# Dropping row tiles in AV slots without scores, and moving two stores to another queue, in a sliding-window attention and GELU kernel

## Chip, cores, metric

One core of a Trainium2 chip. The time is the device time of the core in microseconds (us). A kernel is run several times beside the kernel before on the same chip. A time is the median of a kernel's runs unless a mean is named; "span" is first to last instruction, about 1.7 us less than the time.

## Reference, cut

```python
# q, k, v: (4, 8, 768, 64); n_sink = 4; window = 128
scores = q @ k.transpose(0, 1, 3, 2) / sqrt(64)
keep = (key position < 4) | ((0 <= query - key) & (query - key < 128))
a = softmax(where(keep, scores, -1e9))
x = (a @ v) as (3072, 512)
out = gelu(x @ w_in) @ w_out        # w_in (512, 2048), w_out (2048, 512)
```

## The kernel before

The 3072 rows are worked on in six chunks of 512. While chunk c runs through the two weight matmuls (`gemm1`, `gemm2`), the attention of chunk c + 1 is put between the matmuls of `gemm2`, in slots: scores of two units, then their masks, and four slots later AV (the product of the attention weights with the values) of the two units. A unit is a pair of heads in a group of 256 queries; two groups make a chunk, three groups a batch. Chunk 0 and the attention of chunk 1 are in a hand-made list, the prologue.

AV of two units at once: the window part takes 128 rows of the array. The four sink keys (the first four keys of a batch, which every query sees) are a second, small part per head. For a pair of units it uses row tiles: the array is split into two halves of 64 rows that work at the same time, with unit one's sinks on one half and unit two's on the other. Going from 128 to 64 rows or back is a "mode change" below.

```python
    def av(*units, spare=False, fill=0):
        ets = [ET.pop(u) for u in units]
        pos = [bank2() if spare else bank() for _ in units]
        tiled = len(units) > 1
        ...
        def sinks(n, e):
            g, p = units[n]
            rows = slice(HP * (p // 2), HP * (p // 2 + 1)) if tiled else slice(0, P)
            nc.tensor.matmul(                                     # L526
                pos[n][:, e * PV : (e + 1) * PV],
                lhsT=ETS[g][rows, e * P : (e + 1) * P],
                rhs=VS[g // NBP % 2][rows, 2 * p : 2 * p + 2, :]...
                start=not tiled and e == 0, stop=tiled, ...)
        for n, (g, p) in enumerate(units):
            sunk = g % NBP > 0          # the first group of a batch has no separate sinks
            for e in range(2):
                if sunk and not tiled:
                    sinks(n, e)
                ... four (or three) window matmuls ...            # L546
        if tiled:
            for e in range(2):
                for n, (g, p) in enumerate(units):
                    if g % NBP > 0:
                        sinks(n, e)
        ... per unit: reciprocal (L564), product into xg (L568) on VectorE ...

    def pair_slots(c, weights):
        us = units(c)
        ...
        for n in range(0, len(us), 2):
            two = us[n : n + 2]
            slots[n + 4].append((0, lambda two=two: av(*two)))
            slots[n].append((2, lambda two=two: [scores(*u) for u in two]))   # L473
            slots[n].append((4, lambda two=two: [mask_scores(*u) for u in two]))
```

Eight units a chunk: AV lies in slots 4, 6, 8 and 10, scores in slots 0, 2, 4 and 6. So slots 8 and 10 hold AV alone.

The stores of the last chunk, at the end of `gemm2_mm`:

```python
            eng = nc.scalar if part[0] == DM // 2 else nc.sync
            eng.dma_start(out=out[r0 : r0 + P, cols], in_=osb[:, cols])
```

Row blocks 0 to 2 are stored whole, block 3 in three parts, the middle one from ScalarE's queue.

The softmax here doesn't subtract the row's maximum and nothing guards it: scores larger than these inputs give would overflow.

## Time and profile before

| | before |
|---|---|
| time, median of 3 runs | 226.35 us |
| span of the profiled run | 224.0 us |
| TensorE busy | 97% |
| AV slot without scores, first AV to first L682, earlier / later of a chunk | 0.80 / 0.90 us |
| end wait for the last store to SP's first drain | 0.43 us |

A row of the timeline is a run of equal instructions: start, length, engine, line, tiles, count. TensorE's records overlap, so only differences of starts are durations. The rows themselves are in the prediction.

### The profile page before, as it was taken

What the parts mean: (1) busy time and instruction counts of PE and PEld (TensorE: products, weight loads), DVE (VectorE), ACT (ScalarE), POOL (GpSimd) and SP (SyncE); (2) the same over time, 40 slices, a digit from 0 to 9 for tenths busy, and PEclk for the clock granted to TensorE, in tenths of its full rate; (3) what the DMA queues carried; (4) which work ended last, traced back from release to release, by engine and by line L of the source; (5) the groups of instructions that cost most, each with busy time, mean ns of one, the idle gap of its engine ahead of it and who ended that gap; (6) DMA issues with size and microseconds to landing.
All of it is one profiled execution on the core that took longest, in us unless ns stands there. A gap on an engine that the chain in (4) does not pass through costs nothing.

```text
span 224.0 us, 4231 instructions
## 1 busy us (share of the span) xinstructions
PE 216.8 (97%) x1705; PEld 114.9 (51%) x1705; DVE 111.7 (50%) x267; ACT 120.8 (54%) x148; POOL 51.8 (23%) x95
## 2 busy tenths in 40 slices
PE   7898999999999999999999999999999999999994
PEld 2455887554544465444455444455444465444453
DVE  4437725786690287480297580297550397100121
ACT  2367675866165974065973165963157972278000
POOL 8475513466220011310011400011400011300000
PEclk9999999999999999999999999999999999999999
DMA  6999999999487994477997487986582027500112
GB/s 169 290 348 388 354 352 290 360 273 320 149 188 147 282 276 98 94 151 137 302 255 98 94 171 162 295 217 109 105 170 41 3 47 98 122 17 3 47 47 94
DMA packets 70194, 40.11 MB, mean 179 GB/s; under 512 B 27168, under 2 KB 64416, under 8 KB 70176
## 3 DMA queue, kind: packets, MB, share of 16 engines
q1 hardware_dynamic: 68112, 34.55, 61.0%
q0 software_dynamic: 1920, 5.25, 9.4%
q8 instruction: 13, 0.21, 0.4%
q10 hardware_dynamic: 144, 0.07, 0.1%
q14 instruction: 5, 0.04, 0.1%
HBM read 27.26 MB, written 6.29 MB: 150 GB/s over the span
## 4 chain that ended last, share of the span: by engine, by line
PE 86%; ACT 5%; DVE 3%; DMA 2%; issue 1%; SPq 0%; DVEq 0%
PE po L682 34%; PE big L613 29%; PE bank L546 4%; PE big L473 4%; PE big L646 4%; ACT et L482 3%; DMA st<-in_q_dram 2%; PE po L646 2%; PE bank L613 2%; PE bank L526 1%; ACT L713 1%; DVE xg L568 1%; PE qkps L363 1%; PE big L363 1%; PE big L462 1%
## 5 line engine op out<-in xcount | busy, mean ns | idle before, releaser
L682 PE MATMUL po<-WOUT,gt 128*128 128x512 bf16 (+2 forms) x416 | 89.8, 363 | 0.1
L613 PE MATMUL big<-xt,WIN 128*128 128x512 bf16 x300 | 66.1, 379 | 0.0
L682 PEld LDWEIGHTS <-gt 128*128 128x128 bf16 x416 | 36.9, 98 | 39.5 <-issue 3.0
L632 ACT ACTIVATE gt<-big 128x1024 bf16<-128x1024 f32 (+1 forms) x32 | 30.6, 969 | 44.7 <-PE big L613 44.7
L613 PEld LDWEIGHTS <-WIN 128*128 128x128 bf16 x320 | 31.4, 98 | 37.7
L482 ACT ACTIVATE et<-big 128x1024 bf16<-128x1024 f32 (+1 forms) x48 | 43.4, 952 | 11.7 <-PE big L473 11.5
L697 POOL DMA_DIRECT2D out_dram<-osb x40 | 22.9, 578 | 107.6 <-DVE rz L564 79.8
L490 DVE TENSOR_TENSOR et<-et,mask 128x1024 bf16<-128x1024 bf16 x31 | 22.3, 729 | 33.6 <-ACT et L482 33.2
L272 DVE COPY osb<-po 128x512 f32<-128x512 f32 (+2 forms) x25 | 16.1, 646 | 38.4 <-PE po L682 38.4
L568 DVE TENSOR_TENSOR xg<-bank,rz 128x256 bf16<-128x256 f32 x44 | 18.7, 425 | 1.5
L546 PEld LDWEIGHTS <-et 128*128 128x128 bf16 x352 | 14.6, 97 | 5.0 <-issue 0.2
L272 DVE CAST vo<-st 64x512 bf16<-64x512 f32 x36 | 16.4, 456 | 0.4
L473 PE MATMUL big<-qt,kt 64*128 64x128 bf16 (+1 forms) x256 | 15.5, 238 | 0.8 <-ACT et L482 0.2
L626 ACT ACTIVATE gt<-big 128x1024 bf16<-128x1024 f32 (+1 forms) x8 | 9.8, 1240 | 11.0 <-PE big L613 11.0
L546 PE MATMUL bank<-vo,et 128*128 128x65 bf16 x324 | 14.2, 193 | 0.0
L646 PEld LDWEIGHTS <-WIN 128*128 128x128 bf16 x128 | 12.3, 98 | 1.5
L473 PEld LDWEIGHTS <-kt 64*128 64x128 bf16 x256 | 8.6, 94 | 7.7 <-issue 6.0
L497 DVE TENSOR_TENSOR et<-et,mask 128x768 bf16<-128x768 bf16 x12 | 6.9, 581 | 9.8 <-ACT et L482 9.5
L713 ACT ACT_TABLE_LOAD x9 | 11.5, 1283 | 0.2
L564 DVE RECIPROCAL rz<-bank 128x4 f32<-128x4 f32 x44 | 7.7, 175 | 5.9 <-PE bank L526 3.2
L646 PE MATMUL big<-xt,WIN 128*128 128x256 bf16 x80 | 10.3, 273 | 0.0
L272 DVE CAST k<-st 128x1024 bf16<-128x1024 f32 (+1 forms) x12 | 8.1, 672 | 3.2 <-DMA st<-in_k_dram 3.2
(86 smaller groups left out, 138.2 us busy)
## 6 DMA issues: line engine op xcount, KB each, us to landing
st<-in_k_dram SPq DMA_DIRECT2D x12, 512.0 KB, 7.1
st<-in_q_dram SPq DMA_DIRECT2D x12, 512.0 KB, 7.3
st<-in_v_dram SPq DMA_DIRECT2D x12, 512.0 KB, 7.3
out_dram<-osb POOLq DMA_DIRECT2D x40, 128.0 KB, 2.7
st<-in_moe_w_in_dram SPq DMA_DIRECT2D x8, 512.0 KB, 9.6
st<-in_moe_w_out_dram SPq DMA_DIRECT2D x8, 512.0 KB, 8.9
out_dram<-osb SPq DMA_DIRECT2D x3, 256.0 KB, 2.0
kt<-k SPq DMA_TRANSPOSE x16, 3.0
```

Of the source, the lines that this page charges most:

```text
L272: eng.tensor_copy(out=out, in_=in_)
L473: nc.tensor.matmul(ps[:, hl, c : c + n * P], lhsT=kt(gk, p, ek, rows), rhs=qt(g, p, e, n, rows), start=not add, stop=True, skip_group_chec ...
L482: nc.scalar.activation(out=et[:, :, c0:], in_=ps[:, :, c0:], func=AF.Exp, scale=att_scale)
L490: nc.vector.tensor_tensor(out=et.rearrange("p h (e n) -> p (h e) n", e=2), in0=et.rearrange("p h (e n) -> p (h e) n", e=2), in1=mask.unsqu ...
L546: nc.tensor.matmul(pos[n][:, e * PV + hl * DV : e * PV + (hl + 1) * DV], lhsT=ets[n][:, hl, c : c + P], rhs=vo[:, h, :], start=e == 0 and ...
L568: nc.vector.tensor_tensor(out=XG[g][:, :, 2 * p : 2 * p + 2, :], in0=po[:, 0 : 2 * PV].rearrange("p (e h c) -> p e h c", e=2, h=2)[:, :, : ...
L613: nc.tensor.matmul(outs[a], lhsT=WIN[:, t, ts(f, P)], rhs=XT[c][:, :, t, :], start=(t == 0), stop=(t == NKT - 1),)
L632: nc.scalar.activation(out=gt.rearrange("k a n -> k (a n)"), in_=src, func=AF.Gelu)
L646: nc.tensor.matmul(out4[a], lhsT=WIN[:, t, ts(f, P)], rhs=XT[c][:, 2 * half : 2 * half + 2, t, :], start=(t == 0), stop=(t == NKT - 1), sk ...
L682: nc.tensor.matmul(po, lhsT=GT[c, f // 4][:, f % 4, ts(m, P)], rhs=WOUT[:, f, cols], start=(f == 0), stop=(f == NFT - 1),)
L697: nc.gpsimd.dma_start(out=out[r0 : r0 + P, :].rearrange("(s r) c -> r s c", r=2)[r], in_=osb[HP * r : HP * (r + 1), :],)
L713: nc.scalar.activation(out=warm[:, 1:2], in_=warm[:, 0:1], func=func)
```

## The change

Its intent: in slots with scores the sinks share their change to 64 rows with the scores, which need it too; in slots without, the change of mode stands there for the sinks alone, so drop the row tiles. And move two stores off the hardware queues.

```diff
-    ("s", [3,3], ""), ("av", [3,0,2], ""), ...
+    ("s", [3,3], ""), ("av", [3,0,2], "U"), ...
-    ("av", [3,1,3], ""), ...
+    ("av", [3,1,3], "U"), ...
-            eng = nc.scalar if part[0] == DM // 2 else nc.sync
+            eng = nc.gpsimd if m < 2 else nc.scalar if part[0] == DM // 2 else nc.sync
-            slots[n + 4].append((0, lambda two=two: av(*two)))
+            groups = [two] if n + 4 < len(us) else [[u] for u in two]
+            slots[n + 4].append((0, lambda groups=groups: [av(*us) for us in groups]))
# in run(): an "av" entry marked "U" calls av once per unit, too
```

## The prediction

> **What bounds the kernel now.** I read the page first, then the chain of work that ended last, then the PE timeline round every AV block, last the end of the program. The page:
>
> ```profile
> PE 216.8 (97%) x1705; PEld 114.9 (51%) x1705; DVE 111.7 (50%) x267; ACT 120.8 (54%) x148; POOL 51.8 (23%) x95
> PEclk9999999999999999999999999999999999999999
> PE 86%; ACT 5%; DVE 3%; DMA 2%; issue 1%; SPq 0%; DVEq 0%
> ```
>
> TensorE is busy for 97% of the 224.0 us, holds 86% of the chain, and has its full clock in every slice. So a nanosecond taken out of the PE stream inside chunks 1 to 4 should reach the end, unless another engine then holds PE up. The records overlap (a 128x512 matmul is written as 380 ns but a new one starts every 216 ns), so I work with starts, never with durations. The PE timeline of the first two slots that the change rewrites (AV, no scores):
>
> ```profile
> 84.75 0.65 PE L546 MATMUL bank<-vo,et 128*128 128x65 bf16 x16
> 85.33 0.29 PE L526 MATMUL bank<-vsk,ets 64*128 64x130 bf16 x4
> 85.54 1.90 PE L682 MATMUL po<-WOUT,gt 128*128 128x512 bf16 x8
> 87.28 0.74 PE L546 MATMUL bank<-vo,et 128*128 128x65 bf16 x16
> 87.96 0.29 PE L526 MATMUL bank<-vsk,ets 64*128 64x130 bf16 x4
> 88.18 0.60 PE L682 MATMUL po<-WOUT,gt 128*128 128x512 bf16 x2
> ```
>
> L546 is AV, L526 the sink part of AV on 64 rows, L682 the second matmul of the MoE, on 128 rows. From the first start of L546 to the first of L682 the slot takes 0.80 us, and the later one 0.90 us. For contrast, one of the two slots of chunk 3's loop whose batch has no separate sinks, so that it never leaves 128 rows:
>
> ```profile
> 151.58 0.53 PE L546 MATMUL bank<-vo,et 128*128 128x65 bf16 x12
> 151.94 1.89 PE L682 MATMUL po<-WOUT,gt 128*128 128x512 bf16 x8
> ```
>
> 0.36 us for 12 matmuls: 30 ns each, and nothing lost on either side. Single records of the trace say where the 0.80 goes: starts are 29 to 35 ns apart in AV, then 124 ns from the last AV to the first sink (29 is normal, so 95 lost), 70 ns for four sinks (two and two, partners 3 to 4 ns apart), 149 ns to the first L682 (57 is normal after 130 columns, so 92 lost), and 226 instead of 216 ns inside the first L682: 10 more. In the later slot 128 ns lie between the eighth and the ninth AV. There PE's queue has a separate semaphore instruction of 51 ns: the ninth weight load waits for two engines (DVE and ACT), and one instruction holds one wait.
>
> In the slots that hold scores as well, the switch into 64 rows is shared:
>
> ```profile
> 79.22 0.65 PE L546 MATMUL bank<-vo,et 128*128 128x65 bf16 x16
> 79.80 0.29 PE L526 MATMUL bank<-vsk,ets 64*128 64x130 bf16 x4
> 79.92 0.60 PE L473 MATMUL big<-qt,kt 64*128 64x128 bf16 x12
> 80.46 1.68 PE L682 MATMUL po<-WOUT,gt 128*128 128x512 bf16 x7
> ```
>
> L473 follows L526 after 53 ns, with no loss: the scores would need 64 rows anyway. This is why the change leaves those slots alone.
>
> **What the Trainium skill says.** "TensorEngine Tiling (Array Packing)", Key Properties: "Changing tiling mode (not just tile) drains the TensorE". The trace agrees: 92 to 98 ns lost at every change between 128 and 64 rows, nothing without one. "TensorE: Matmul & The Clock Gate", Part 3: matmuls in different row tiles run at the same time, starts about 4 ns apart. The trace agrees with 3 to 4 ns; that concurrency is what the change gives up. "Perfetto Trace Analysis", Sequencer-only Instruction: such a record starts when its semaphores are satisfied, the wait itself is not in it. The trace agrees: the end wait for the last store starts at 222.60 us, its last increment lands at 222.59. I use this below.
>
> **The change, part by part.** (1) The untiled pair. The early untiled pair of the same kernel, in the prologue, is the ruler:
>
> ```profile
> 24.04 0.22 PE L526 MATMUL po<-vsk,ets 128*128 128x130 bf16 x1
> 24.09 0.28 PE L546 MATMUL po<-vo,et 128*128 128x65 bf16 x4
> 24.21 0.22 PE L526 MATMUL po<-vsk,ets 128*128 128x130 bf16 x1
> ...
> 24.74 0.28 PE L588 MATMUL bank<-ident,xg 128*128 128x128 bf16 x2
> ```
>
> From 24.04 to 24.74 us: 0.706 us by the single records, for 4 sinks at 57 and 16 AV at 30 ns. So the instruction count stays, the sinks cost 228 instead of 70 ns, and both switches go. The earlier slot goes from 799 + 10 to 706, a gain of 0.103 us. In the later one the built program's double wait is gone too (the sink's load takes the DVE wait, the AV load the ACT wait): 895 + 10 to 706, a gain of 0.199 us. Together 0.302 us a chunk.
>
> How many chunks: the rule is all slots from the fifth unit on, in the loops that prepare chunks 2 to 5. Those are the second groups, 5, 7, 9 and 11. Group 9 starts a batch (9 is a multiple of 3) and has no separate sinks; its order in the built program is the same before and after. So three chunks, at 84.7, 117.8 and 184.4 us: 3 x 0.302 = **0.91 us**. The two marked prologue entries are of group 3, also a batch start: no TensorE or DVE instruction moves, worth 0. Groups whose prologue AV does lose two switches (44.45 and 48.61 us) are left tiled.
>
> (2) The two stores. Where they run is nothing: they leave at 211 and 214 us and have landed by 216.5. But completion semaphores of the hardware queues go round in eight lanes, and SP waits for the lanes in fixed order at the end. Its end records and waits:
>
> ```profile
> L869 SPq EVENT_SEMAPHORE  x11: 17/28/28, 221.4 to 223.9; - x11
> L869 SPq DRAIN  x3: 7/7/13, 223.0 to 223.4; - x3
> SPq L869 <- DMA out_dram<-osb: 1.1, 2, 0.7
> ```
>
> The built program shows the last store on lane 1 before, the third of nine waits. In the trace it ends at 222.60; six waits that have long been satisfied follow one after the other, 61 ns each (222.668, .729, .789, .850, .909, .971), and only then the drain at 223.036. With two stores fewer on the hardware queues the last store has lane 7, the ninth wait: the others are done while it is in flight. Worth 6 x 61 = **0.37 us**, all at the end of the chain.
>
> Sum: 0.91 + 0.37 = 1.28 us, from 226.35 to **225.1 us**, 0.57%.
>
> **The rivals.** (a) The bank takes the switch's place. In the later slot the second unit needs the bank that DVE's xg of the slot before frees; that ends at 87.473, set by ACT's exp and DVE's mask and copy, which do not move. A PE wait on such an xg started 53 ns after its end at 153.8, so the load can start at 87.526; PE would come at 87.53. It just fits. If it did not, 0.05 us in each of three chunks: 225.2. (b) The PE gain is absorbed at a chunk's edge. The first matmul there needs xg's DMA transpose: issued 89.50, some 3.1 us to landing, so 92.6 against a start at 93.15. The change brings xg forward by about 0.5 us, as unit by unit DVE starts earlier, and PE by 0.3, so the slack grows. PE does wait for ACT at the head of a chunk (L473, 0.13 to 0.39 us), but that ACT chain (last Gelu, table load, two exps) starts at PE's last first-matmul and moves with it. Against this rival, then; if true, only the tail is left, 226.0. (c) The stores hurt. GpSimd's stores take 2.7 us to landing against 1.8 on SP, and its drain lasted 4.27 us after its last store. From 214.1 us that ends near 218.4, over 3 us before the last landing. A third store would have come close, two do not. If it were wrong, some 1 us is lost: 226. (d) The end waits stay in the chain although the lane changes: then 225.4.
>
> **Range and chances.** The terms come from the same trace with starts that repeat within 3 ns in three chunks; the three runs before spread by 0.35 us, more than any term's doubt. With (a), (d) and the spread, 224.7 to 225.7 should hold it. 2% would be 4.5 us, over three times what I can find, and nothing that the change adds costs as much: faster by over 2% 0.01, within 2% 0.98, slower 0.01.
>
> **What would show it.** Right: in the PE timeline the six slots start with L526 on 128 rows and take 0.70 to 0.72 us to the first L682; the PE chain arrives 0.3 us earlier after each of three chunks and not after chunk 3's loop; the span falls to about 222.7; the last store's end wait is followed by the drain within 0.1 us. Wrong: a gap before the second unit's sink in the later slot (a); PE waits longer at L613 or L473 at chunk heads (b); a GpSimd semaphore or GpSimd itself comes last at the end (c); six 61 ns steps still after the last landing (d).

## The result, and the profile after

| | before | after |
|---|---|---|
| median of 6 runs | 226.32 us | 224.99 us |
| lowest to highest | 225.66 to 226.73 | 224.48 to 225.75 |
| span of the profiled run | 224.0 us | 223.6 us |
| AV slots without scores | 0.80 / 0.90 us | 0.71 / 0.71 to 0.72 us |
| end wait for the last store to first drain | 0.43 us | 0.07 us |

The ratio is 0.9945, with a 95% interval of 0.9919 to 0.9971: about 1.25 us less, where 1.28 was predicted; the interval reaches from 0.7 to 1.8 us. A ratio is the mean time of one kernel's runs over that of the other's of the same rounds, so not quite the ratio of the medians quoted.

The PE timeline of the same two slots after (the first two that the change rewrites):

```profile
85.59 0.22 PE L526 MATMUL bank<-vsk,ets 128*128 128x130 bf16 x1
85.64 0.28 PE L546 MATMUL bank<-vo,et 128*128 128x65 bf16 x4
...
86.30 1.89 PE L682 MATMUL po<-WOUT,gt 128*128 128x512 bf16 x8
88.02 0.22 PE L526 MATMUL bank<-vsk,ets 128*128 128x130 bf16 x1
...
88.74 0.81 PE L682 MATMUL po<-WOUT,gt 128*128 128x512 bf16 x3
```

L526 now reads 128*128: the whole array. 85.59 to 86.30 and 88.02 to 88.74 are 0.71 and 0.72 us. The six slots took 708, 717, 709, 713, 711 and 714 ns by the single records; before they took 799, 895, 799, 892, 799 and 893. With the first L682 at 216 to 217 instead of 226 to 227 ns, that is 0.87 us saved, where 0.91 was predicted.

The end of the program after, in the rows of the end line and of SP's waits (count, shortest, median and longest in ns, first and last start):

```profile
L875 SPq EVENT_SEMAPHORE  x11: 17/28/28, 221.4 to 223.5; - x11
L875 SPq DRAIN  x3: 7/7/13, 222.6 to 223.0; - x3
SPq L875 <- DMA out_dram<-osb: 0.7, 1, 0.7
```

SP waits once for a store, not twice, and its first drain, at 223.0 before, is at 222.6. By the single records the nine waits start at 221.38, then in steps of some 61 ns to 221.82, and the last one, lane 7, at 222.584; the drain follows at 222.649. TensorE's last matmul started at 220.45 before and 220.43 after, so nearly all of the 0.4 us by which these two profiled spans differ is this end.

That is the puzzle of this pair of traces: TensorE saved 0.87 us in its slots, yet reached its end at the same moment. Where it was given back is in a part of the prologue that the change does not touch. The timeline near 44 us, before:

```profile
43.48 0.69 DVE L490 TENSOR_TENSOR et<-et,mask 128x1024 bf16<-128x1024 bf16 x1 [0.43 <-ACT et L482]
43.94 0.70 PE L546 MATMUL bank<-vo,et 128*128 128x65 bf16 x16
44.50 1.04 POOL L272 CAST WOUT<-st 128x1024 bf16<-128x1024 f32 x1 [1.15 <-DMA st<-in_moe_w_out_dram]
```

and after:

```profile
42.10 2.38 POOL L272 CAST WOUT<-st 128x1024 bf16<-128x1024 f32 x2 [2.26 <-DMA st<-in_moe_w_out_dram]
43.62 1.40 DVE L490 TENSOR_TENSOR et<-et,mask 128x1024 bf16<-128x1024 bf16 x1 [0.43 <-ACT et L482]
44.08 0.41 PE L546 MATMUL bank<-vo,et 128*128 128x65 bf16 x8
45.07 0.41 PE L546 MATMUL bank<-vo,et 128*128 128x65 bf16 x8 [0.58 <-DVE et L490]
```

GpSimd casts weights when their load lands. In the run before, the second of these casts came after DVE's mask (44.50). In the run after, its load landed earlier (43.32 us, against 44.45 before), and the cast ran from 43.44 to 44.48, when the mask started at 43.62. The mask then took 1.40 instead of 0.69 us, and AV of group 2 waited for it between its eighth and its ninth matmul (776 ns between their starts, 72 before). The first L613 after the prologue starts at 59.995 instead of 59.148: 0.85 us late. From there the starts of the later chunks tell the gain: 93.151 became 93.706 (0.29 won), 126.207 became 126.475 (0.29), 159.018 became 159.287 (nothing, as predicted for that chunk), 192.798 became 192.779 (0.29). Two of the six runs after had a span of 222.8, which is what the prediction's 222.7 asks for; the profiled one was not among them.

"SBUF — State Buffer", section Who interferes with whom, of the Trainium skill states that a DVE instruction with two inputs in SBUF and a GpSimd instruction that reads SBUF exclude each other, and that the second to start waits for the first to end. The traces agree in both directions: mask first (before, 41.76), the cast takes 1.38 instead of 1.04 us; cast first (after, 43.44), the mask takes 1.40 instead of 0.69.

### The profile page after: what moved, and what is told of

It is laid out like the page before. It is cut to its first block, busy times and chain, and to the rows that moved or that the text cites.

```text
span 223.6 us, 4228 instructions
## 1 busy us (share of the span) xinstructions
PE 215.2 (96%) x1705; PEld 114.7 (51%) x1705; DVE 112.8 (50%) x267; ACT 120.8 (54%) x148; POOL 52.3 (23%) x97
## 4 chain that ended last, share of the span: by engine, by line
PE 85%; ACT 5%; DVE 4%; DMA 2%; issue 1%; SPq 0%; DVEq 0%
PE po L682 34%; PE big L613 29%; PE bank L546 4%; PE big L473 4%; PE big L646 4%; ACT et L482 3%; DMA st<-in_q_dram 2%; PE po L646 2%; PE bank L613 2%; PE bank L526 1%; ACT L715 1%; DVE et L490 1%; DVE xg L568 1%; PE qkps L363 1%; PE big L462 1%
## 5 line engine op out<-in xcount | busy, mean ns | idle before, releaser
L682 PE MATMUL po<-WOUT,gt 128*128 128x512 bf16 (+2 forms) x416 | 89.8, 364 | 0.1
L613 PE MATMUL big<-xt,WIN 128*128 128x512 bf16 x300 | 66.1, 379 | 0.0
L682 PEld LDWEIGHTS <-gt 128*128 128x128 bf16 x416 | 36.9, 98 | 38.9 <-issue 3.0
L613 PEld LDWEIGHTS <-WIN 128*128 128x128 bf16 x320 | 31.3, 98 | 37.8
L568 DVE TENSOR_TENSOR xg<-bank,rz 128x256 bf16<-128x256 f32 x44 | 18.7, 424 | 1.5
L546 PEld LDWEIGHTS <-et 128*128 128x128 bf16 x352 | 15.2, 97 | 4.9 <-DVE et L490 0.7
L546 PE MATMUL bank<-vo,et 128*128 128x65 bf16 x324 | 15.1, 193 | 0.6 <-DVE et L490 0.6
```

The costliest lines, as they stand in the source:

```text
L546: nc.tensor.matmul(pos[n][:, e * PV + hl * DV : e * PV + (hl + 1) * DV], lhsT=ets[n][:, hl, c : c + P], rhs=vo[:, h, :], start=e == 0 and ...
L568: nc.vector.tensor_tensor(out=XG[g][:, :, 2 * p : 2 * p + 2, :], in0=po[:, 0 : 2 * PV].rearrange("p (e h c) -> p e h c", e=2, h=2)[:, :, : ...
L613: nc.tensor.matmul(outs[a], lhsT=WIN[:, t, ts(f, P)], rhs=XT[c][:, :, t, :], start=(t == 0), stop=(t == NKT - 1),)
L682: nc.tensor.matmul(po, lhsT=GT[c, f // 4][:, f % 4, ts(m, P)], rhs=WOUT[:, f, cols], start=(f == 0), stop=(f == NFT - 1),)
```

## The experiments

Twelve runs, all correct.

**1. Each half alone, and tiles dropped everywhere.** `e1_slots_only` is the change without its store line:

```diff
-            eng = nc.gpsimd if m < 2 else nc.scalar if part[0] == DM // 2 else nc.sync
+            eng = nc.scalar if part[0] == DM // 2 else nc.sync
```

> The slot half of the change alone, the stores as before. My theory (six slots without scores lose their two row-mode changes, three of them also the double wait): 0.91 us less than the kernel before, the six slots at 0.70 to 0.72 us from the first sink to the first L682, and six satisfied waits of 61 ns still standing after the last landing. Rival (the gain comes mainly from the stores): within 0.3 us of before.

Measured: ratio 0.9959 (0.9944 to 0.9974), 0.93 us less than before by the ratio; the six slots took 709 to 718 ns. The single records still show the last store's wait at 221.965, six more of some 61 ns, and the drain at 222.398: 0.43 us. As the theory says.

`e2_stores_only` is the kernel before with only the store line changed:

```diff
-            eng = nc.scalar if part[0] == DM // 2 else nc.sync
+            eng = nc.gpsimd if m < 2 else nc.scalar if part[0] == DM // 2 else nc.sync
```

> The store half alone, the slots as before. My theory (the last store moves from lane 1 to lane 7, so six end waits of 61 ns are done while it flies): 0.37 us less than before, all of it between the last landing and the first drain (0.43 us before, 0.07 us after). Rival (the stores do nothing): 0.0 us and 0.43 us in that place.

Measured: ratio 0.9982 (0.9967 to 0.9997), 0.41 us less by the ratio. From the last store's wait (223.438) to the drain (223.503) 0.07 us. The two halves add up: 0.93 + 0.41 = 1.34 against 1.25 for both, within the intervals.

`e3_lanes_split`, on the kernel before, asks whether GpSimd has anything to do with it:

```diff
-            eng.dma_start(out=out[r0 : r0 + P, cols], in_=osb[:, cols])
+            for w0 in range(part[0], part[0] + part[1], P if m < 2 else part[1]):
+                cs = slice(w0, w0 + (P if m < 2 else part[1]))
+                eng.dma_start(out=out[r0 : r0 + P, cs], in_=osb[:, cs])
```

> The kernel before, no store on GpSimd; the first two stores of the last chunk are cut into four each on the sync queue, so that six more hardware DMAs turn the last store to lane 7. If the lane alone is the cause: the same 0.37 us as the stores half, 0.07 us from the last landing to the first drain. Rival (GpSimd's queue or a shorter sync queue is the cause): no gain, or a loss from eight issues of 0.33 us.

Measured: the profile did what the lane theory says (its rows of the end line and of SP's waits):

```profile
L871 SPq DRAIN  x3: 7/7/7, 223.3 to 223.6; - x3
SPq L871 <- DMA out_dram<-osb: 0.7, 1, 0.7
```

The last store's wait is at 223.214, the drain at 223.279: 0.07 us, without any store on GpSimd. But the ratio was 1.0007 (0.9994 to 1.0021): no gain in time. Its profiled run, at a span of 224.2, is explained: the prologue's AV stall was there (694 ns), and 224.0 + 0.61 (its first L613 at 59.758) - 0.40 gives 224.2. The five other runs had 224.5 to 224.8, more than that, and nothing of them but the span is known. So the cause of the missing gain was open; run `e12_split_stores` and point 5 below take it up.

`e4_untile_all`, on the changed kernel, drops the tiles in all pairs:

```diff
-            groups = [two] if n + 4 < len(us) else [[u] for u in two]
+            groups = [[u] for u in two]
-                for two in [[u] for u in us] if "U" in op[2] else [us]:
+                for two in [[u] for u in us]:
```

> The changed kernel with every AV pair untiled, also in the slots that hold scores. My theory (there the row tiles share their mode change with the scores): the six such slots with sinks in the loops go from 0.70 us (first AV to first score) to about 0.80 us, 0.097 us each or 0.58 us in all; the two pairs of group 2 in the prologue gain 0.1 us each; so some 0.4 us slower than the changed kernel, about 0.9 us faster than before. Rival (untiled AV is simply faster anywhere): a further 0.5 us gain over the changed kernel.

Measured: ratio 0.9967 (0.9953 to 0.9982), 0.85 us under before by the means (0.75 by the ratio), so some 0.4 us of the change's 1.25 us was lost (the changed kernel itself did not run on this chip). Its PE timeline of a slot with scores:

```profile
78.95 0.22 PE L526 MATMUL bank<-vsk,ets 128*128 128x130 bf16 x1
...
79.54 0.28 PE L546 MATMUL bank<-vo,et 128*128 128x65 bf16 x4
79.75 0.61 PE L473 MATMUL big<-qt,kt 64*128 64x128 bf16 x12
```

From the first AV instruction to the first score 0.80 us; with tiles (79.22 to 79.92 in the kernel before) it was 0.70. By the single records 805 to 807 ns in all six such slots with sinks, 702 to 705 with tiles. The mode change does not go away, it moves in front of the scores, and the sinks lose their concurrency. Untiled AV is not faster as such; the rival falls.

**2. Is it the mode change, or only the order unit by unit?** `e6_tiles_one_by_one`, on `e1_slots_only`, keeps the units apart in these slots, but with row tiles:

```diff
-        tiled = len(units) > 1
+        tiled = rowtile or len(units) > 1
-            ... [av(*us) for us in groups]
+            ... [av(*us, rowtile=True) for us in groups]   # rowtile: new argument of av, False otherwise
```

(The flag reaches the slots with scores as well; their pairs are tiled anyway.)

> The kernel before, in the slots without scores each unit of the pair alone, but still with row tiles: four mode changes a slot instead of two, and no two sinks at the same time. My theory (about 95 ns for each change, 57 ns for a sink alone): each unit takes 207 + 124 + 57 + 149 = 537 ns, so 1.08 us from the first AV to the first L682 in the earlier slot (0.80 before) and 1.17 in the later one, which keeps its double wait (0.90 before); over six slots 1.65 us slower than before. Rival (the gain of the change is one of order, unit by unit, and not of the modes): faster than before by up to 0.9 us.

Measured: ratio 1.0058 (1.0038 to 1.0079), 1.3 us slower. The later slot of the first pair of slots in its PE timeline:

```profile
87.58 0.40 PE L546 MATMUL bank<-vo,et 128*128 128x65 bf16 x8
87.91 0.28 PE L526 MATMUL bank<-vsk,ets 64*128 64x130 bf16 x2
88.13 0.42 PE L546 MATMUL bank<-vo,et 128*128 128x65 bf16 x8
88.48 0.28 PE L526 MATMUL bank<-vsk,ets 64*128 64x130 bf16 x2
88.70 0.39 PE L682 MATMUL po<-WOUT,gt 128*128 128x512 bf16 x1
```

1.12 us. In the earlier slot the trace lacks one matmul's record; counted in, it is 1.12 as well. TensorE's last matmul started 1.61 us later than in the kernel before, with the same prologue (first L613 at 59.128 and 59.148); 1.65 was expected. The time grew by less than that, as more of the runs before than of these lay in the longer group of spans (experiment 3). The parts were a little off: a sink alone took 66 to 68 ns on 64 rows, not 57, and the double wait, still in the built program, cost nothing here: the ninth AV follows its sink after 149 ns in both slots, the same as a mode change without it. The record shows why: the separate semaphore instruction of the later slot ran at 87.489 us, 39 ns after the end of the xg that it waits for, and so before even the first AV of its slot (87.577). It was done long before PE reached the ninth AV.

**3. The prologue.** Four runs on one chip. `e5_after_again` is the changed kernel.

> The changed kernel again, as the ruler for the three runs beside it. Expected 1.28 us under the kernel before. My theory for its spread (0.8 us wide, as wide as that of the kernel before): in the prologue a mask of DVE (two inputs in SBUF) meets a GpSimd cast of weights, which starts whenever its load lands; whichever starts first blocks the other, and where the cast was first, AV of group 2 waits up to 0.7 us for its second unit. So the gap between the eighth and the ninth AV near 44 us should be one of 0.03 to 0.8 us, and large just where a cast started before the mask did. Rival (the spread is noise of the clock or of the end): no such gap goes with a long run.

Measured: ratio 0.9954 (0.9935 to 0.9973). The six spans fell into two groups: 222.7 and 222.8, and four times 223.6. The profiled run was one of the long ones, with 775 ns before the ninth AV, and again its cast (43.43) started before the mask (43.61), which took 1.40 us. The nine profiles with uncut casts agree with the expectation: in the five where a cast was well under way when the mask of group 2 began (changed kernel, `e1_slots_only`, `e2_stores_only`, `e3_lanes_split`, this one) the gap was 246 to 780 ns; in the other four, where the cast came later, had ended, or was in its last 0.1 us (`e4_untile_all`), it was at most 90.

`e7_untile_group2` takes the change one step further, in the two places that the prediction had named as left out:

```diff
-    ("av", [2,0,2], ""), ... ("av", [2,1,3], "")
+    ("av", [2,0,2], "U"), ... ("av", [2,1,3], "U")
```

> The changed kernel, with the two AV pairs of group 2 in the prologue untiled as well; they stand between weight matmuls, without scores. My theory: each loses two mode changes, 0.80 + 0.01 to 0.71 us, together 0.20 us less than the changed kernel. Rival (the prologue is bound by loads, DVE or ACT there, and the gain is given back at once): the first L613 after the prologue starts no earlier, 0.0 us.

Measured: ratio 0.9933 (0.9916 to 0.9949), means 0.54 us under `e5_after_again`. Spans 222.4, 222.5, 222.5 and 223.0 to 223.2. Its PE timeline of the two pairs:

```profile
43.97 0.22 PE L526 MATMUL bank<-vsk,ets 128*128 128x130 bf16 x1
...
44.68 1.03 PE L682 MATMUL po<-WOUT,gt 128*128 128x512 bf16 x3
...
48.04 0.22 PE L526 MATMUL bank<-vsk,ets 128*128 128x130 bf16 x1
...
48.75 0.38 PE L682 MATMUL po<-WOUT,gt 128*128 128x512 bf16 x1
```

0.71 us each, where the kernel before took 0.85 and 0.80. In this trace, as in that of the kernel before, the cast came after the mask, and the two are alike up to 44 us: the first L613 starts at 58.924 against 59.148, 0.22 earlier. So the 0.20 foreseen is there; the shorter group of spans, 222.4 to 222.5 against 222.7 to 222.8, says the same. The rest of the 0.54 between the means may be how many runs fell into the longer group (three of six against four).

`e8_quarter_casts`, on the changed kernel, cuts the three late casts:

```diff
-            copy(eng, WOUT[:, j * NW : (j + 1) * NW, :], st.rearrange("p (f c) -> p f c", c=DM))
+            ... for j in (4, 5, 6) four copies of [128, 256], else as before
```

> The changed kernel, with the three late weight casts of GpSimd cut into four quarters each (256 instead of 1024 elements, so about 0.3 instead of 1.04 us). If a mask is blocked for as long as the GpSimd instruction that was there first: no mask of the prologue after 40 us takes over 1.1 us (1.4 before), the gap before the ninth AV stays under 0.4 us, and the runs' spread falls to about half, the mean 0.2 to 0.4 us under the changed kernel. Rival (GpSimd and DVE share in small steps, so that only the total overlap counts): masks as long as before, no change in the spread.

Measured: ratio 0.9954 (0.9933 to 0.9974). In the timeline the mask of group 2 met a quarter and waited for that quarter only:

```profile
41.85 5.65 POOL L272 CAST WOUT<-st 128x256 bf16<-128x256 f32 x12 [1.65 <-DMA st<-in_moe_w_out_dram]
43.56 0.81 DVE L496 TENSOR_TENSOR et<-et,mask 128x1024 bf16<-128x1024 bf16 x1 [0.42 <-ACT et L488]
```

0.81 us, with a gap of 189 ns before the ninth AV: what "blocked for as long as the instruction that was there first" asks for, and not what sharing in small steps would give. But the run did not show the smaller spread: four spans of 222.8 to 223.1, and two of 223.7 and 224.2; the mean (224.99) is that of `e5_after_again` (225.05). The block is shown. It is not the whole of the spread: in the profile of `e11_sync_stores` below, with the same cut casts and at most 88 ns between two AV of group 2, the first gemm1 matmul still came at 60.24 us, 1.35 us later than in that of `e9_quarters_group2` (58.89). There TensorE itself waited twice for weights that GpSimd had still to cast:

```profile
47.95 0.59 PE L688 MATMUL po<-WOUT,gt 128*128 128x512 bf16 x2 [0.53 <-POOL WOUT L272]
49.04 0.59 PE L688 MATMUL po<-WOUT,gt 128*128 128x512 bf16 x2 [0.50 <-POOL WOUT L272]
```

The load behind these casts landed at 46.27, in `e9_quarters_group2` at 45.34.

`e9_quarters_group2` has both edits, those of `e7_untile_group2` and `e8_quarter_casts`, on the changed kernel.

> Quarters of the casts and group 2 untiled together, on the changed kernel: the candidate that should beat both kernels. Sum of the two expectations: 0.4 to 0.6 us under the changed kernel, 1.7 to 1.9 us under the kernel before, so about 224.4 us. If the two gains lie on the same wait, only the larger of them.

Measured: ratio 0.9932 (0.9916 to 0.9947), median 224.41, spans 222.5 to 222.8 and one of 223.3. It beats both kernels: 1.52 us under the kernel before and 0.56 under the changed kernel beside it (means), at the top of the range expected for the second, short of it for the first. It is no better than `e7_untile_group2` (mean 224.49 against 224.51), so the quarters are worth nothing that these runs can show, and the simpler of the two is to be preferred.

**4. The end again, on `e9_quarters_group2`.** `e11_sync_stores` puts all stores back as they were before; `e12_split_stores` cuts the first two as `e3_lanes_split` did; `e10_three_stores` has `m < 3` in place of `m < 2`.

```diff
 # e11_sync_stores
-            eng = nc.gpsimd if m < 2 else nc.scalar if part[0] == DM // 2 else nc.sync
+            eng = nc.scalar if part[0] == DM // 2 else nc.sync
 # e12_split_stores: that line as in e11, and the loop of e3_lanes_split around the store
 # e10_three_stores
-            eng = nc.gpsimd if m < 2 else ...
+            eng = nc.gpsimd if m < 3 else ...
```

> On the same kernel: all three whole stores back on the sync queue, last store on lane 1. Expected 0.37 us slower than with two stores on GpSimd (mean 224.49 then), 0.43 us from last landing to first drain.

Measured: ratio 0.9956 (0.9935 to 0.9976), 0.43 us from the last store's wait (222.838) to the drain (223.270), as expected. Its mean of 225.17 is 0.68 us above that of `e9_quarters_group2`, where 0.37 was expected, but on another chip, and two of its six spans (223.9 and 224.2, the others 223.1 to 223.2) were long; its profile is one of them.

> On the same kernel: no store on GpSimd, the first two stores cut into four each on the sync queue, last store on lane 7. The first run of this kind on the kernel before showed 0.07 us from last landing to drain as foreseen, yet no gain in time (+0.1 us, where -0.37 was expected). If that was the prologue's spread, this run is 0.37 us faster than the run beside it with whole stores on the sync queue. If cutting the stores costs 0.4 us somewhere, it is the same as that run, and its profile must show the place.

Measured: ratio 0.9934 (0.9911 to 0.9957), the mean 0.49 us under `e11_sync_stores` beside it; 0.07 us from wait (222.069) to drain (222.134). That is what the lane's gain without GpSimd should look like, but the two intervals overlap, so the time alone does not show it; point 5 does. In the profiled run the last store itself landed 1.82 us after it was issued, 0.26 us more than the 1.56 in the changed kernel's profile. Such a late landing could have hidden part of the gain in the unprofiled runs of `e3_lanes_split`, but no run shows that it did, and those runs stay unexplained.

> On the kernel with quarter casts and group 2 untiled: a third store on GpSimd. My theory: the last store now has lane 6, so one satisfied wait follows it, 0.06 us more than with two stores. GpSimd's drain, which ended 4.05 us after its last store began (214.69 to 218.74), would end near 221.4, just short of the last landing near 221.5: no more cost, but no room left. Rival: the drain comes last and the end moves out by 0.5 us or more.

Measured: ratio 0.9951 (0.9930 to 0.9972). The last store's wait (lane 6) starts at 221.854, one wait and 0.13 us later comes the drain. GpSimd's own drain ended at 221.486, 0.37 us before that: no cost, as expected, and no room left. The time differs from that of `e9_quarters_group2` by more than the 0.06 us expected, but on another chip and within the spread that the prologue makes, so nothing follows from it.

**5. All traces between the same two marks.** The two marks are the first gemm1 matmul after the prologue (L613, or L619 where casts are cut) and TensorE's last matmul. They split each profiled span, in us:

| run | to the first gemm1 | from there to the last matmul | from there to the end |
|---|---|---|---|
| before | 59.15 | 161.30 | 3.54 |
| `e2_stores_only` | 59.98 | 161.31 | 3.16 |
| `e3_lanes_split` | 59.76 | 161.30 | 3.15 |
| `e1_slots_only` | 59.37 | 160.44 | 3.52 |
| after | 60.00 | 160.44 | 3.17 |
| `e11_sync_stores` | 60.24 | 160.45 | 3.52 |
| `e12_split_stores` | 59.21 | 160.45 | 3.42 |

Every trace with the slot change as it stands, also those of `e5_after_again`, `e7_untile_group2`, `e8_quarter_casts`, `e9_quarters_group2` and `e10_three_stores`, has 160.44 to 160.45 us in the middle: some 0.86 us less than before, whatever the prologue did. The end is shorter by 0.37 to 0.39 us wherever the last store has lane 7, without GpSimd too (`e3_lanes_split`); only `e12_split_stores` loses 0.26 us of it to its late landing. All the rest of the spread between these profiles lies before the first gemm1. A prologue as late as that of `e11_sync_stores` would put `e3_lanes_split` at 224.7 us (an estimate: 60.24 + 161.30 + 3.15), the span of its slower runs; no run shows that it had one.

## Why the prediction was right

Its sum, 1.28 us, met 1.25, and not by two errors that cancel: the traces give 0.87 in the slots and 0.37 at the end, 1.24 us. That the times agree within 0.03 is luck, as their interval is 0.7 to 1.8 us, and the repeat (`e5_after_again`) gave 1.04 by its ratio. By its own steps:

- *Two mode changes a slot, 0.103 us:* 0.10 us in each of the three earlier slots. Doubling the changes made it worse by what was expected (`e6_tiles_one_by_one`); dropping the tiles where the change cannot be saved made it worse too (`e4_untile_all`). The cause is shown.
- *The double wait, 0.096 us in the later slots:* all three later slots came down from 892 to 895 ns to 713 to 717. The size was right, but the cause named was half of the cause. The source view of L546 in the kernel before, and the last row of DVE ahead of the ninth AV:

```profile
L546 PEldq EVENT_SEMAPHORE  x4: 51/51/51, 51.5 to 187.2; - x4
87.05 0.42 DVE L568 TENSOR_TENSOR xg<-bank,rz 128x256 bf16<-128x256 f32 x1
```

By the single records the separate semaphore instruction starts at 87.512, 120.570 and 187.161 us, each time 39 to 40 ns after the end of the DVE product (xg, L568) that frees the second unit's bank. A record of this kind starts when its semaphore is satisfied, as the prediction itself reads the end waits. So TensorE was waiting for the bank, and the second wait lengthened that: the weight load follows the xg's end after 115 ns, where a load with a single wait follows after 53 (153.8 us). With a single wait the ninth AV would have come about 0.01 us late instead of 0.098 (an estimate from these starts). Where TensorE came to the second unit later than that, the same instruction cost nothing (`e6_tiles_one_by_one`).
- *The untiled length, 706 ns:* 708 to 717. The ruler from the prologue was good to about 0.01 us. This also bounds rival (a): the bank was free just in time, as the margin of zero said. In all three later slots the load of the second unit's first sink starts 53 to 54 ns after the xg's end (88.370 after 88.316, for one), at a cost of at most 9 ns. Anything that shortens the first unit further would meet this wait.
- *Three chunks and not four:* the starts of L613 advanced by 0.29, 0.29, 0 and 0.29 us.
- *Rival (b), loss at a chunk's edge:* none; each chunk's 0.29 was still there at the next first matmul.
- *The prologue's marked pairs, 0:* the built program's order there is unchanged.
- *The end, 0.37 us:* 0.369 in the profiled pair (last matmul to end of span, 3.54 and 3.17 us), 0.41 by time in `e2_stores_only`. That the lane is the cause, and not GpSimd, is shown by the single records of `e3_lanes_split` and `e12_split_stores` and by the end of the first of them, 3.15 us; the unprofiled times of `e3_lanes_split` don't show it, and that stays open.
- *Rivals (c) and (d):* GpSimd's drain ended at 218.74, 3.8 us before the last landing; the six waits ran during the flight. (The 4.27 us in the prediction are the length of the drain's own record, 194.41 to 198.68; from the start of the last store, at 194.50, it is 4.18.)

One statement of it failed: "the span falls to about 222.7" in the profile. It was 223.6. The step behind it, that the runs' spread is just a doubt to be added at the end, left out that much of the spread has a place. A wait of 0.7 us in the prologue comes and goes with the arrival of one load, and the profiled run of before was without it, that of after with it. For the same reason "0.3 us earlier after each of three chunks" holds only against the first L613. The traces of two kernels have to be compared from a common mark (here the first L613), not by their spans alone.

## What to carry to other kernels

Small matmuls in row tiles pay when their neighbours run in the same mode; alone between full-array matmuls, a pair of sinks saved 158 ns by running two at a time and paid 190 for two mode changes. Look at what stands before and after, not at the matmul. At the end of a program, look at what is still done after the last store has landed: here six waits that had long been satisfied. At a wait record, ask first when its semaphore was set: an extra wait instruction cost time here only where the awaited result came at the last moment. And where runs spread more than the term you look for, compare their traces from a common mark before you add the spread to the error bar.

## What the Trainium skill lacked or had wrong

- "TensorEngine Tiling (Array Packing)", Key Properties, says that a change of tiling mode drains the array, without a figure: here 92 to 98 ns for each change between 128 and 64 rows, in either direction.
- I found in no page I read what a second semaphore wait costs an instruction on TensorE: a separate record of 51 ns, and 115 instead of 53 ns from the end of the awaited DVE instruction to the weight load where that end came last; nothing where it came early enough (149 ns after a mode change with it and without).
- "DMA: Bandwidth & Descriptors", Issuing engines are not separate DMA queues, says that issuing from several engines only saves sequencer time. Here it moved the last store to another completion semaphore, and the order of the end waits, 61 ns each, made that worth 0.37 us.
- I found in no page I read how long GpSimd's drain lasts after its last store began: 4.05 to 4.18 us (214.69 to 218.74 in the changed kernel, 217.36 to 221.49 with three stores, 194.50 to 198.68 before). It limits how late a store may leave from GpSimd.
- "SBUF — State Buffer", Who interferes with whom, was right, in both orders (1.40 instead of 0.69 us for the mask, 1.38 instead of 1.04 us for the cast).
